# Fused attention and gated feed-forward on one core: V and K loads of two batches issued later in the second chunk

## The chip, the core and the metric

The kernel runs on 1 of the 8 cores of one Trainium2 chip. Its five engines work side by side and meet only at semaphores: TensorE (matmuls; PE in the profile), VectorE (DVE), ScalarE (ACT), GpSimd (POOL) and SyncE (SP). The last three issue DMAs too, each through a queue of its own (q0 GpSimd, q1 SyncE, q10 ScalarE), all run by the same 16 DMA engines. The metric is the device time of one execution, in microseconds (us).

## What is computed

Attention with a causal mask and a decay from running sums, for 8 batches, 8 heads, 576 positions and 64 elements per head; then RMS norm and a gated feed-forward layer over 4608 tokens of 512 elements, with an inner width of 1536.

```python
scores = scale * np.matmul(q, k.transpose(0, 1, 3, 2))
cum = np.cumsum(np.maximum(s, 0.0), axis=-1)
bias = -(cum[:, :, :, None] - cum[:, :, None, :])
scores = np.where(causal, -1000000000.0, scores + np.minimum(bias, 0.0))
...
attn = attn / (np.sum(attn, axis=-1, keepdims=True) + 1e-09)
x = np.matmul(attn, v)            # to (4608, 512): tokens of a batch follow each other
...
g = (x / rms * rms_g) @ w_gate
return (g * (1.0 / (1.0 + np.exp(-g))) * ((x / rms * rms_g) @ w_val)) @ w_out
```

The kernel looks only at the key block of a query block and the one before it (weights further off are below its tolerance; it checks this, and a second, general path is there if the check fails).

## The kernel before

**Two streams, woven by hand.** The feed-forward layer works in 9 chunks of 512 tokens (`ffn`, L746). A chunk has 12 pairs of gate matmuls (L756) and value matmuls (L765), four of 128x512 each, and then four output tiles of twelve matmuls (L778). The attention of batch b must give its normed, turned tokens (`xnT`) before the chunk that holds them. To fill TensorE, attention work is placed between the groups of the chunk's matmuls: after each group `step()` (L681) is called, 36 times a chunk, and a running number, `slot`, counts the calls. `phase()` is the number within the chunk. Chunk 1, the stretch of this case, has slots 37 to 72.

**What a step records.** First the second half of the last score group's exponentials (`pending`); then scaling and the transpose of a finished x block by DMA (`x_scale`, L386; `xt_dma`, L394); one entry of the ScalarE list (`act_side`); one DMA transpose of keys or queries (`kq_dma`, L170); on odd slots one entry of the V list (`v_side`); one of the GpSimd list (`pool_side`); then, by `place()`, scores (`s_step`), attention times V (`av_step`) or a transpose on TensorE (`t_step`); then a check entry on VectorE. Each list is served from its head: an entry is a pair of a condition and the work. The order on each engine is the order of recording; nothing is reordered later. An engine that runs ahead of the others starts what was recorded for later steps, as far as its semaphores let it.

**How a batch's data arrive.** Keys and queries come as float32 in one DMA of 1 MB for 512 rows (`load_kq`, L127, line L129) and one of 128 KB for the last 64 rows (`load_kq_tail`, L133, line L135), issued by ScalarE, into one buffer for keys and one for queries (`kq32`). They are cast to bf16 into `kqn` by GpSimd or ScalarE (L143, L145, L154, L156). For batch 2 the keys are turned on TensorE (L195), the queries by five DMA transposes on SyncE (L182), one for each block. Scores of key block kb read the query blocks kb and kb + 1 (L276, `kqTx[..., kb:kb + 2, ...]`); their matmul is L278, the exponential L302, the causal mask on GpSimd L311. V comes in five blocks (four of 128 rows, one of 64), each one DMA that GpSimd issues, with a cast to bf16 (`load_v`, L184, line L186), into one of two buffers by the parity of the batch. Attention times V of query block qb reads V blocks qb - 1 and qb (L344, L350) and is divided on VectorE (L357, L359); the norm's sum is taken on ScalarE (L366) and its power on GpSimd (L379, L382), the scaling on VectorE (L389), the transpose to `xnT` by SyncE (L400).

**Who sets the moved loads' places.** `over(w)` (L509) is recorded with the last cast of batch b and lists the next batch's load on `act_side`, by `early` with a lag of 4 slots. With `loads` (L486) the bulk and the tail are also 3 slots apart from each other and from the load before. `after_av(b)` (L549) runs when batch b's attention is finished and lists V of batch b + 2: for b = 0 three entries that wait for chunk 1, otherwise one entry a block by `early`, with a lag of 6 slots. The entry `done["V", b]` only tells the scheduler from when on attention of that batch may be placed.

**Slots before**, as the schedule gives them: V of batch 2 blocks 0 and 1 at 37, 2 and 3 at 39, 4 at 41; queries of batch 3 (bulk) at 40, tail at 43; query transposes of batch 2 at 37, 39, 42, 44, 46; V of batch 3 at 45, 47, 49, 51, 53; keys of batch 3 at 46, tail at 49, their five casts at 56 to 60; scores of batch 2 at 46 (key block 0, heads 0 to 3), 49, 52 (key block 1, heads 0 to 3), 55 and on.

Of the kernel before, what the change touches and what calls it, by code (L numbers as in the profile page):

```python
# [26 lines left out]
def kernel(  # L27
# [19 lines left out]
    NSC = 5  # L47
# [6 lines left out]
    def rows(c):  # L54
        return 128 if c < 4 else 64
# [71 lines left out]
    def load_kq(eng, b, w, h0=0, h1=H):  # L127
        src = k if w == 0 else q
        eng.dma_start(  # L129
            out=kq32[:, w, h0:h1, 0:256],  # L130
            in_=src[b, h0:h1, 0:512, :].rearrange("h (p r) d -> p h (r d)", r=4))

    def load_kq_tail(eng, b, w):  # L133
        src = k if w == 0 else q
        eng.dma_start(  # L135
            out=kq32[0:64, w, :, 256:320],
            in_=src[b, :, 512:576, :].rearrange("h p d -> p h d"))

    def cast(eng, b, w, r0, r1, h0=0, h1=H):
        o = kqn[:, b % 2, w, r0:r1, h0:h1, :]  # L140
        i = kq32[:, w].rearrange("p h (r d) -> p r h d", d=D)[:, r0:r1, h0:h1, :]
        if eng is nc.scalar:
            eng.activation(out=o, in_=i, func=AF.Copy)  # L143
        else:
            eng.tensor_copy(out=o, in_=i)  # L145

    def cast_x(eng, b, w, hp):

        if hp < HP:
            o = kqn[:, b % 2, w, 0:4].rearrange("p r h d -> p (r h d)")[:, hp * 512:hp * 512 + 512]  # L150
            o = o.rearrange("p (r h d) -> p h r d", r=4, h=2)
            i = kq32[:, w, 2 * hp:2 * hp + 2, 0:256].rearrange("p h (r d) -> p h r d", d=D)
            if eng is nc.scalar:
                eng.activation(out=o, in_=i, func=AF.Copy)  # L154
            else:
                eng.tensor_copy(out=o, in_=i)  # L156
        else:
            cast(eng, b, w, 4, 5)

    def load_k(b, c):  # L160
        n = rows(c)
        nc.gpsimd.dma_start(
            out=kqn[0:n, b % 2, 0, c],
            in_=k[b, :, c * 128:c * 128 + n, :].rearrange("h p d -> p h d"))
# [19 lines left out]
    def load_v(b, c):  # L184
        n = rows(c)
        nc.gpsimd.dma_start(  # L186
            out=v_sb[0:n, b % 2, c, :, 0:64],
            in_=v[b, :, c * 128:c * 128 + n, :].rearrange("h p d -> p h d"))
# [243 lines left out]
    SLOTS = 36  # L432
    K2 = 34
    slot = [0]
    first, chunk = [0], [0]
    done = {}
# [10 lines left out]
    pool_side, dve_side, v_side, act_side = [], [], [], []  # L447
# [5 lines left out]
    def ready(lag, *key):  # L453
        return at(*key) + lag <= slot[0]
# [11 lines left out]
    def early(queue, lag, fns):  # L466

        t = slot[0] + lag
        queue.extend((lambda: slot[0] >= t and phase() < 24, f) for f in fns)

    def check(b, ws=(1, 0)):
        t = slot[0] + (8 if b >= KB else 0)

        def when(w):
            if b < 2:
                return slot[0] % 2 and chunk[0] == b and slot[0] > 16
            return phase() >= 25 and slot[0] >= t and (w == 0 or ready(0, "cast", b, 1))
        dve_side.extend((lambda w=w: when(w), f) for w in (ws if b < KB else (0, 1)) for f in (
            lambda w=w: check_mag(b, w), lambda: check_max(0), lambda: check_max(1),
            lambda w=w: done.__setitem__(("check", b, w), slot[0])))  # L480

    def phase():

        return slot[0] - first[0]

    def loads(b, w, when, lag):  # L486

        def main():
            load_kq(nc.scalar, b, w)
            last["L"] = slot[0]  # L490

        def tail():
            load_kq_tail(nc.scalar, b, w)
            done["raw", b, w] = last["L"] = slot[0]
        n = len(act_side)
        when(act_side, lag, [main, tail])
        act_side[n:] = [(lambda c=c: c() and slot[0] - last["L"] >= 3, f) for c, f in act_side[n:]]

    def casts(b):

        def key(c):
            load_k(b, c)
            done["K", b, c] = slot[0]
            if c == NSC - 1:
                check(b)

        def over(w):  # L509
            done["cast", b, w] = slot[0]  # L510
            if b + 1 < B and (w == 1 or b + 1 < KB):
                loads(b + 1, w, early, 4)
            if w == 1:
                x_seq.extend((b, ww, c) for c in range(NSC) for ww in ((1, 0) if b >= KB else (1,)))
            else:
                done["cast", b] = slot[0]
                check(b)

        def free(w):
            return ready(0, "check", b - 2, w) and (  # L520
                ready(0, "T", b - 2) if w == 0 and b < KB + 2 else
                b < XB + 2 or ready(4, "X", b - 2, w, 4))
        if b >= KB:
            pool_side.extend((lambda: free(0) and slot[0] % 2 == 0, lambda c=c: key(c)) for c in range(NSC))
        fns = [(1, lambda r=r: cast_x(nc.gpsimd, b, 1, r)) for r in range(NSC)]
        if b == 2:
            fns[-1] = (1, lambda: (cast_x(nc.gpsimd, b, 1, NSC - 1), over(1)))
        else:
            fns += [(1, lambda: over(1))]
        if b < KB:  # L530
            fns += [(0, lambda r=r: cast(nc.gpsimd, b, 0, r, r + 1)) for r in range(NSC)]
            fns += [(0, lambda: over(0))]
        if b == 2:

            def put2(queue, t, *fs):
                queue.extend((lambda: slot[0] >= t and free(0) and free(1), f) for f in fs)
            put2(act_side, K2, *[lambda r=r: cast_x(nc.scalar, b, 1, r) for r in (3, 4)])
            put2(act_side, K2 + 3, *[lambda r=r: cast(nc.scalar, b, 0, r, r + 1) for r in (0, 1, 2)])
            put2(pool_side, K2, *[lambda r=r: cast_x(nc.gpsimd, b, 1, r) for r in (0, 1)],
                 lambda: (cast_x(nc.gpsimd, b, 1, 2), over(1)),  # L540
                 lambda: cast(nc.gpsimd, b, 0, 3, 4), lambda: (cast(nc.gpsimd, b, 0, 4, 5), over(0)))
            return
        pool_side.extend((lambda w=w: ready(7, "raw", b, w) and free(w), f) for w, f in fns)
# [5 lines left out]
    def after_av(b):  # L549
        if b + 2 < B:  # L550
            if b == 0:
                v_side.extend((lambda: chunk[0] == 1, f) for f in (
                    lambda: (load_v(2, 0), load_v(2, 1)), lambda: (load_v(2, 2), load_v(2, 3)),
                    lambda: (load_v(2, 4), done.__setitem__(("V", 2), slot[0]))))
                return
            early(v_side, 6, [lambda r=r: load_v(b + 2, r) for r in range(NSC)]
                  + [lambda: done.__setitem__(("V", b + 2), slot[0])])

    def in_av(b, hp):
# [29 lines left out]
    def do_av(key, ps=None, act=False, apart=False):  # L589
        b, qb, g = key  # L590
        act = act or b > 1 or b == 1 and qb > 1
        norm = av_step(b, qb, g, ps, act)
        if g == 1 and not apart:
            norm()
        done["AV", b, qb, g] = slot[0]
        last["AV"] = slot[0]
        last["AVT" if b > 0 and g == 1 else "AVA"] = slot[0]
        if qb == 4 and g == 1:
            if b == 0:
                nc.vector.memset(v_sb[:, 0, :, :, 64:65], 1.0)  # L600
            after_av(b)
        return norm
# [638 lines left out]
```

## Time and profile before

| what | us |
|---|---|
| median of 3 runs | 365.74 |
| lowest and highest of them | 365.17, 367.58 |
| the profiled execution | 365.71 |
| its span | 364.1 |

How to read the rows: a page row of an engine has its busy time, its share of the span and the number of instructions. A row of the order of time has the start, the length, the engine (with a small q: its queue's issuing instruction), the line, the operation, output <- input, sizes, the count, and in brackets the idle time before it and what ended it. An answer for one line gives shortest, median and longest duration in ns, then the first and last start. A row of a DMA queue gives its packets, MB, and the time of its packets as a share of 16 engines over the window. Matmuls are pipelined, so the bars of neighbouring groups overlap a little.

### The profile page before, as it was taken

Reading aid. Unit: us, or ns where it says so; the run is one execution under the profiler, and the core shown is the slowest. Engines: PE = TensorE matmul, PEld = TensorE weight load, DVE = VectorE, ACT = ScalarE, POOL = GpSimd, SP = SyncE. Lnnn points to the kernel's source line nnn. Section 1 sums busy time; section 2 is a strip of 40 time slices with the busy share of each in tenths; the row PEclk is TensorE's granted clock in tenths of the full one; section 3 lists DMA queues with packets and bytes.
Section 4 is the critical chain, followed back from the end, with each engine's and each line's share of the span. In section 5 each row is a group of like instructions: output and inputs, shape, how many; then the busy total and the mean of one; then the engine's idle time right before and its main releaser. Section 6 shows DMA issues by size and latency. Waiting matters only on the chain. (4 is left out here: it accounts for less than half of the span.)

```text
span 364.1 us, 6986 instructions
## 1 busy us (share of the span) xinstructions
PE 349.6 (96%) x2387; PEld 161.2 (44%) x2387; DVE 272.7 (75%) x524; ACT 240.8 (66%) x619; POOL 174.1 (48%) x281
## 2 busy tenths in 40 slices
PE   5989999998999999999999999999999999999993
PEld 2445444543444444444444444444444444444441
DVE  6697988696887889789988889884588558827820
ACT  3988885776787877876778767777677644223311
POOL 7959763747856465979648833722232200000000
PEclk9999999999999999999999999999999999999998
DMA  7999999999979299999979944952200130020011
GB/s 233 135 222 256 174 176 252 176 196 176 199 133 137 40 199 119 199 161 158 162 213 160 140 109 117 114 78 70 90 14 17 43 110 1 0 88 29 1 58 63
DMA packets 124800, 45.68 MB, mean 125 GB/s; under 512 B 103924, under 2 KB 119800, under 8 KB 124760
## 3 DMA queue, kind: packets, MB, share of 16 engines
q0 software_dynamic: 62368, 13.11, 48.0%
q1 hardware_dynamic: 51328, 23.67, 31.3%
q10 hardware_dynamic: 11064, 8.41, 9.9%
q8 instruction: 19, 0.31, 0.4%
q14 instruction: 21, 0.17, 0.2%
HBM read 37.90 MB, written 9.44 MB: 130 GB/s over the span
## 5 line engine op out<-in xcount | busy, mean ns | idle before, releaser
L302 ACT ACTIVATE E<-psS,biasK 128x256 bf16<-128x256 f32 (+3 forms) x328 | 107.3, 412 | 23.1 <-PE psS L278 21.8
L756 PE MATMUL psF<-xnT,wg_sb 128*128 128x512 bf16 x432 | 111.1, 380 | 0.3 <-ACT xnT L416 0.3
L765 PE MATMUL psF<-xnT,wv_sb 128*128 128x512 bf16 x432 | 111.1, 379 | 0.0
L778 PE MATMUL psF<-wout_sb,Ht 128*128 128x512 bf16 x432 | 102.3, 379 | 0.0
L768 DVE SCALAR_TENSOR_TENSOR U<-T,psF 128x512 bf16<-128x512 f32 x108 | 73.7, 682 | 29.4 <-ACT T L759 29.0
L759 ACT ACTIVATE T<-psF 128x512 f32<-128x512 f32 x108 | 64.4, 596 | 41.4 <-PE psF L756 39.1
L311 POOL TENSOR_SCALAR_AFFINE_SELECT E<-E 128x512 bf16<-128x512 bf16 x64 | 44.6, 697 | 86.6 <-ACT E L302 86.4
L761 DVE TENSOR_TENSOR Ht<-U,psF 128x512 bf16<-128x512 bf16 x99 | 67.7, 684 | 7.0
L756 PEld LDWEIGHTS <-wg_sb 128*128 128x128 bf16 x432 | 38.6, 98 | 44.5 <-issue 5.8
L778 PEld LDWEIGHTS <-Ht 128*128 128x128 bf16 x432 | 38.8, 98 | 42.6 <-issue 2.3
L765 PEld LDWEIGHTS <-wv_sb 128*128 128x128 bf16 x432 | 38.6, 98 | 42.2 <-issue 4.0
L783 ACT ACTIVATE osb<-psF 128x512 f32<-128x512 f32 x36 | 21.5, 598 | 33.3 <-PE psF L778 27.7
L389 DVE SCALAR_TENSOR_TENSOR xs_sb<-x_sb,al_all,g_row 128x512 bf16<-128x512 bf16 (+1 forms) x36 | 29.1, 808 | 13.1 <-POOL al_all L382 12.4
L186 POOL DMA_DIRECT2D v_sb<-in_v_dram x40 | 34.9, 875 | 0.2 <-PE psF L756 0.2
L366 ACT ACTIVATE xs_sb<-x_sb 128x512 bf16<-128x512 bf16 (+1 forms) x37 | 23.5, 636 | 10.9 <-DVE x_sb L359 10.4
L278 PE MATMUL psS<-kqT 64*128 64x256 bf16 (+2 forms) x304 | 25.9, 256 | 2.8 <-DMA kqT<-kqn 1.6
L350 PEld LDWEIGHTS <-E 128*128 128x128 bf16 x320 | 21.7, 97 | 10.1 <-issue 0.2
L427 DVE TENSOR_TENSOR acc<-acc,mag 128x1280 bf16<-128x1280 bf16 x32 | 26.0, 831 | 0.2
L382 POOL TENSOR_TENSOR al_all<-al_all,mhalf 128x1 f32<-128x1 f32 (+2 forms) x39 | 22.2, 570 | 3.3
L278 PEld LDWEIGHTS <-kqT 64*128 64x128 bf16 x320 | 9.0, 94 | 32.9 <-issue 30.5
L344 PEld LDWEIGHTS <-E 128*128 128x128 bf16 x256 | 20.0, 98 | 7.7 <-DVE x_sb L359 0.6
L379 POOL TENSOR_SCALAR al_all<-ss_all 128x1 f32<-128x1 f32 (+2 forms) x39 | 10.3, 263 | 26.3 <-ACT xs_sb L366 18.2
(124 smaller groups left out, 302.4 us busy)
## 6 DMA issues: line engine op xcount, KB each, us to landing
out_dram<-osb SPq DMA_DIRECT2D x36, 256.0 KB, 2.3
kq<-in_q_dram ACTq DMA_DIRECT2D x5, 1024.0 KB, 6.1
v_sb<-in_v_dram POOLq DMA_DIRECT2D x32, 128.0 KB, 6.6
kq<-in_k_dram SPq DMA_DIRECT2D x4, 512.0 KB, 5.4
kq<-in_q_dram SPq DMA_DIRECT2D x4, 512.0 KB, 7.5
kq<-in_k_dram ACTq DMA_DIRECT2D x2, 1024.0 KB, 12.8
kqn<-in_k_dram POOLq DMA_DIRECT2D x16, 128.0 KB, 5.9
wout_sb<-in_moe_w_out_dram POOLq DMA_DIRECT2D x2, 768.0 KB, 10.1
```

The source lines that it names most:

```text
L186: nc.gpsimd.dma_start(out=v_sb[0:n, b % 2, c, :, 0:64], in_=v[b, :, c * 128:c * 128 + n, :].rearrange("h p d -> p h d"))
L278: nc.tensor.matmul(pair[par][:, j * W:j * W + M], lhsT=kT, rhs=qT, start=(j == 0 and not premask), stop=(j == nj - 1))
L302: nc.scalar.activation(out=eo, in_=ei, func=AF.Exp, scale=0.125, bias=biasK[:, kb, bh:bh + 1])
L311: nc.gpsimd.affine_select(out=Ev[:, :, 0:nq], in_=Ev[:, :, 0:nq], pattern=[[0, nh], [1, nq]], compare_op=ALU.is_ge, fill=0.0, base=0, chan ...
L389: nc.vector.scalar_tensor_tensor(out=xs_sb[0:n, (b * NSC + qb) % NX, :], in0=x_sb[0:n, (b * NSC + qb) % NX, :], scalar=al_all[0:n, col:col ...
L427: nc.vector.tensor_tensor(out=acc[:, sl], in0=acc[:, sl], in1=mag[:, sl], op=ALU.max)
L756: nc.tensor.matmul(Gp, lhsT=wg_sb[:, cc, fs], rhs=xnT[:, cc, x0:x0 + DM], start=(cc == 0), stop=(cc == CC - 1))
L759: nc.scalar.activation(out=T, in_=Gp, func=AF.Tanh, scale=0.5)
L761: nc.vector.tensor_tensor(out=Ht[:, fb - 1, :], in0=pend[0], in1=pend[1], op=ALU.mult)
L765: nc.tensor.matmul(Vp, lhsT=wv_sb[:, cc, fs], rhs=xnT[:, cc, x0:x0 + DM], start=(cc == 0), stop=(cc == CC - 1))
L768: nc.vector.scalar_tensor_tensor(out=U, in0=T, scalar=1.0, in1=Gp, op0=ALU.add, op1=ALU.mult)
L778: nc.tensor.matmul(Op, lhsT=Ht[:, fb, tb * 128:(tb + 1) * 128], rhs=wout_sb[:, fb, :], start=(fb == 0), stop=(fb == FB - 1))
```

## The change

Three places in the scheduler's lists, no change to what is computed. The load of keys of batch 3 gets a lag of 11 slots instead of 4. V of batch 3 gets a lag of 11 instead of 6. V of batch 2 goes in four entries instead of three: blocks 0 and 1, and block 2, from the start of chunk 1; blocks 3 and 4 each alone, once the slot is over SLOTS + 8 = 44. The mark that lets attention of batch 2 be placed is set with block 2.

```diff
-                loads(b + 1, w, early, 4)
+                loads(b + 1, w, early, 11 if (b, w) == (2, 0) else 4)
...
             if b == 0:
-                v_side.extend((lambda: chunk[0] == 1, f) for f in (
-                    lambda: (load_v(2, 0), load_v(2, 1)), lambda: (load_v(2, 2), load_v(2, 3)),
-                    lambda: (load_v(2, 4), done.__setitem__(("V", 2), slot[0]))))
+                v_side.extend((lambda n=n: slot[0] > SLOTS + n, f) for n, f in (
+                    (0, lambda: (load_v(2, 0), load_v(2, 1))),
+                    (0, lambda: (load_v(2, 2), done.__setitem__(("V", 2), slot[0]))),
+                    (8, lambda: load_v(2, 3)), (8, lambda: load_v(2, 4))))
                 return
-            early(v_side, 6, [lambda r=r: load_v(b + 2, r) for r in range(NSC)]
+            early(v_side, 11 if b == 1 else 6, [lambda r=r: load_v(b + 2, r) for r in range(NSC)]
```

The schedule then gives: V of batch 2 block 2 still at slot 39, block 3 at 45 (before 39), block 4 at 47 (41); V of batch 3 at 49, 51, 53, 55, 57 (45 to 53); keys of batch 3 at 49 (46), tail at 52 (49), their casts at 59 to 63 (56 to 60). No other slot changes: the order of instructions on TensorE, VectorE and SyncE is the same in both kernels.

## The prediction

> **What bounds the kernel now.** I read the page first (busy time by engine), then what TensorE waited for, then the orders of time of TensorE, the queues and GpSimd around the one stretch that the change touches.
>
> ```profile
> PE 349.6 (96%) x2387; PEld 161.2 (44%) x2387; DVE 272.7 (75%) x524; ACT 240.8 (66%) x619; POOL 174.1 (48%) x281
> ```
>
> TensorE is busy for 349.6 of the span of 364.1 us; the next engine, VectorE, for 272.7. So a time is won where TensorE stands still, and lost where something makes it stand still. Its waits, longest first (engine, line, what it waited for: us in total, times, longest):
>
> ```profile
> PE psS L247 <- POOL mneg L887: 4.0, 1, 4.0
> PE psS L278 <- DMA kqT<-kqn: 1.6, 1, 1.6
> PE psS L278 <- ACT E L302: 0.6, 1, 0.6
> ```
>
> The 4.0 us lie in the start-up. The 1.6 us are the only wait on a DMA: a score matmul (L278) waits for a turned block of queries or keys (kqT). The order of time of TensorE shows where:
>
> ```profile
> 83.42 1.02 PE L765 MATMUL psF<-xnT,wv_sb 128*128 128x512 bf16 x4
> 86.08 0.39 PE L278 MATMUL psS<-kqT 64*128 64x256 bf16 x4 [1.64 <-DMA kqT<-kqn]
> 92.10 0.39 PE L278 MATMUL psS<-kqT 64*128 64x256 bf16 x4 [0.64 <-ACT E L302]
> 108.67 1.03 PE L756 MATMUL psF<-xnT,wg_sb 128*128 128x512 bf16 x4
> ```
>
> The value matmuls end at 83.42 + 1.02 = 84.44; the scores of batch 2, key block 1, heads 0 to 3 start at 86.08. 108.67 is the first matmul of chunk 2. These scores read query blocks 1 and 2 (L276). Block 2 is the late one; it is the first of three transposes here, behind x of batch 1:
>
> ```profile
> 74.26 1.17 SPq L400 DMA_TRANSPOSE xnT<-xs_sb  x1
> 75.53 4.12 SPq L182 DMA_TRANSPOSE kqT<-kqn  x3
> ```
>
> The answers for one issue alone: x at 74.3, then query block 2 at 75.5 (who waited, and the time from issue to landing), then a transpose of little traffic at 105.1 for comparison:
>
> ```profile
> L400 SPq DMA_TRANSPOSE xnT<-xs_sb x1: 1173/1173/1173, 74.3 to 74.3; - x1
> DMA to landing us min/median/max: 8.0/8.0/8.0
> ...
> L182 SPq DMA_TRANSPOSE kqT<-kqn x1: 1293/1293/1293, 75.5 to 75.5; - x1
>   PE psS L278: 1.6, 1
> DMA to landing us min/median/max: 10.4/10.4/10.4
> ...
> L400 SPq DMA_TRANSPOSE xnT<-xs_sb x1: 1213/1213/1213, 105.1 to 105.1; - x1
> DMA to landing us min/median/max: 2.4/2.4/2.4
> ```
>
> x landed at 74.26 + 8.0 = 82.3, query block 2 at 75.53 + 10.4 = 85.9, which is the wait's end. A transpose can take 2.4 us. What shares the 16 DMA engines with these, by queue (q0 GpSimd's, q1 SyncE's, q10 ScalarE's), from 75.5 to 82.2 and from 82.2 to 86:
>
> ```profile
> q0 software_dynamic: 2949, 0.37, 109.1%
> q10 hardware_dynamic: 1202, 0.80, 55.8%
> q1 hardware_dynamic: 546, 0.13, 19.3%
> ...
> q10 hardware_dynamic: 343, 0.35, 52.7%
> q1 hardware_dynamic: 833, 0.20, 52.7%
> q0 software_dynamic: 567, 0.07, 33.0%
> ```
>
> The transposes are starved up to 82.2 (19.3% of 16 engines) and then share: in the last 3.8 us they need 0.527 x 3.8 = 2.0 us of all engines, the loads of q0 and q10 take 0.857 x 3.8 = 3.3 us.
>
> **The change part by part.** The orders of TensorE, VectorE and SyncE stay what they are; only places on GpSimd and ScalarE move. The rows of these two:
>
> ```profile
> 72.81 3.39 POOL L186 DMA_DIRECT2D v_sb<-in_v_dram  x4
> 81.00 0.63 POOL L311 TENSOR_SCALAR_AFFINE_SELECT E<-E 128x512 bf16<-128x512 bf16 x1 [4.80 <-ACT E L302]
> 83.69 0.63 POOL L311 TENSOR_SCALAR_AFFINE_SELECT E<-E 128x512 bf16<-128x512 bf16 x1 [0.31 <-ACT E L302]
> 88.88 0.63 POOL L311 TENSOR_SCALAR_AFFINE_SELECT E<-E 128x512 bf16<-128x512 bf16 x1 [2.00 <-ACT E L302]
> ...
> 77.37 0.44 ACTq L129 DMA_DIRECT2D kq<-in_k_dram  x1
> 81.39 0.60 ACTq L135 DMA_DIRECT2D kq<-in_k_dram  x1
> ```
>
> (1) V loads. The four at 72.81 are blocks 2, 3, 4 of batch 2 and block 0 of batch 3. GpSimd runs ahead of the steps in which its work was recorded, so what a load is moved past counts, not the step. Block 3 of batch 2 is recorded six steps later, yet nothing with a wait comes to stand before it: it still goes out at 73.8. Block 4 (64 rows) and V 0 of batch 3 come behind the causal mask that waits at 81.00, so they go out at about 81.6 and 82.3 instead of 74.6 and 75.3. V 1 to 4 of batch 3 each move back by one or two masks or casts, to between 85 and 93.
>
> Three landings, block 3 of batch 2 (out at 73.8), V 0 of batch 3 (75.3), K of batch 3 (77.4):
>
> ```profile
> L186 POOL DMA_DIRECT2D v_sb<-in_v_dram x1: 881/881/881, 73.8 to 73.8; - x1
> DMA to landing us min/median/max: 8.4/8.4/8.4
> ...
> L186 POOL DMA_DIRECT2D v_sb<-in_v_dram x1: 905/905/905, 75.3 to 75.3; - x1
> DMA to landing us min/median/max: 14.5/14.5/14.5
> ...
> L129 ACTq DMA_DIRECT2D kq<-in_k_dram x1: 441/441/441, 77.4 to 77.4; - x1
> DMA to landing us min/median/max: 14.1/14.1/14.1
> ```
>
> (2) K of batch 3 (1 MB, L129) moves on ScalarE's queue from 77.37 to the place of its own tail, 81.39; the tail (L135) to behind the next tanh, about 83.6. The issue costs ScalarE nothing that TensorE waits for: 0.4 us of its queue, as before.
>
> (3) The sum. Where do the moved 1.5 V blocks and K stand in the two stretches? Block 3 of batch 2, unmoved, lands at 73.8 + 8.4 = 82.2, so up to there q0 is occupied with or without block 4 and V 0; and on q10 the queries of batch 3, unmoved, stand ahead of K. So x of batch 1 may land as late as before, 82.3, and I credit nothing there. From 82.2 on, q0's and q10's 3.3 us are almost all moved work, which is now issued at 81.4 to 82.3. The transpose of 105.1 took 2.4 us from issue to landing; I take 1.5 to 2 of these, an estimate, as the way to the first packet, so the moved loads begin at about 83 to 84. The transposes' own 2.0 us in that stretch hold block 2 and, behind it, part of the next: run alone from 82.3, block 2 would be through at 84.3 at the latest, and sooner by what of the 2.0 us is the next block's. TensorE is there at 84.44. Bounds: landing before 84.44 removes the whole 1.64 us; landing at 85.9 as now removes nothing. The nearest row, the transpose of 105.1 with its 2.4 us, lies on the early side, and about half of the 2.0 us runs before the first moved packet; I take a residue of 0.1 us, so 1.5 us gained. A price below nothing belongs to the rivals.
>
> The Trainium skill, DMA: Bandwidth & Descriptors, section Queues, rings and completion order, says that each DMA engine goes round-robin between the queues that have work, a packet at a time, and keeps order within one queue. It speaks against the change up to 82.2: a V block that stood behind others on q0 took no turn from the transposes, so taking it out would give nothing there. The 19.3% against 109.1% is no even share, so the trace bears out the turns only from 82.2 on (52.7% each for q1 and q10).
>
> (4) What comes next. With the stall gone everything behind 84.44 moves 1.64 us earlier. The next TensorE wait, 0.64 us at 92.10, is on ScalarE's exponentials, which themselves follow TensorE (scores, tanh), so it moves along and stays. GpSimd: its 2.00 us of idle time at 88.88 shrinks to about 0.4. It has the same loads and casts to do, so it is at most 1.1 us late on masks whose readers come later than that. Block 4 of batch 2 and V of batch 3 are first read in chunk 2, behind 108.67: no reader is near.
>
> The profiled execution took 365.71 us (span 364.1 and 1.6 around it) and the median of the three is 365.74, so nothing has to be converted: 365.7 - 1.5 = **364.2 us**.
>
> **The rivals.** *A, the loads catch the transpose anyway.* If block 2 isn't through when K and V begin at about 83.3, it shares again and lands between 84.9 and 85.9, and the wait keeps 0.5 to 1.5 us: 365.2 to 365.7. For it: the slow landings of the other queues' loads (14.1 us) show engines far behind the mean, and a landing is that of the slowest of 16. Against it: before, x and block 2 shared all the way with V 4 and V 0, and were 3.6 us apart; now 1 us of that is free of them.
>
> *B, slower: K comes late for its casts.* K of batch 3 took 14.1 us; from 81.39 the same gives 95.5. Its first cast now stands on GpSimd behind a V load and one mask. The rows of GpSimd, VectorE and SyncE around it:
>
> ```profile
> 94.37 0.63 POOL L311 TENSOR_SCALAR_AFFINE_SELECT E<-E 128x512 bf16<-128x512 bf16 x1
> 97.34 1.20 POOL L145 CAST kqn<-kq 128x512 bf16<-128x512 f32 x1
> 102.81 0.80 POOL L379 TENSOR_SCALAR al_all<-ss_all 128x1 f32<-128x1 f32 x1 [0.89 <-ACT xs_sb L366]
> 104.27 0.75 DVE L389 SCALAR_TENSOR_TENSOR xs_sb<-x_sb,al_all,g_row 128x512 bf16<-128x512 bf16 x1 [0.72 <-POOL al_all L382]
> 105.05 1.21 SPq L400 DMA_TRANSPOSE xnT<-xs_sb  x1
> ```
>
> That mask ends at 95.0 now, so at 93.4 shifted, and GpSimd would stand about 2 us in front of a mask, the norm of block 1 of batch 2, three casts of 0.6 to 1.2 us each and the norm of block 2 (102.81). This last one sets the chunk's end: x of block 2 is scaled at 104.27, goes out at 105.05, lands 2.4 later at 107.5, and chunk 2 starts at 108.67: 1.2 us of room. With K at 95.5 the norm of block 2 would be 0 to 1.6 us late, so TensorE would wait 0 to 0.4 us. From there each us of K costs one. The kernel is slower than before once K lands later than about 97.5 (16 us after its issue); at 98.5 the time is 366.7. For it: all five V loads of batch 3 now fall into its time. Against it: the queries of batch 3 and block 3 of batch 2, which ran ahead of it and beside it, are nearly through when it starts, so it should take less than 14.1 us.
>
> *C, more than the stall.* The 0.64 us at 92.10 goes too: 365.7 - 1.64 - 0.64 = 363.4. Nothing in the profile says why it should.
>
> **How the numbers follow.** The forecast (the wait goes, all but 0.2 us at most) 0.66; A 0.18; B with a loss against before 0.11; C 0.05. The range leaves out C's lower end and the far part of B: 363.5 to 366.1; the likeliest case's own is 363.8 to 364.7. A measurement of this kernel tells about 1%, 3.7 us, from no change; all cases lie within that except a far B or a gain with no row behind it: faster 0.02, same 0.95, slower 0.03.
>
> **What would show it.** The wait of L278 on kqT gone from TensorE's waits, or below 0.2 us; query block 2 landing before 84.4; V 4 and V 0 issued after the first mask of batch 2 at about 81.6, V 3 still at 73.8; K out at about 81.4; no new TensorE wait on a DMA, on xnT (L756) or on kqT of batch 3; the first matmul of chunk 2 near 107.1. I would be wrong if block 2 still lands after 85 (A), if GpSimd is idle at L145 until K lands and TensorE waits at L756 (B), or if the gain is made in chunk 1 and given back later.

## The result, and the profile after

The changed kernel takes 364.21 us (median of 22 runs, 363.39 to 365.89); the kernel before, timed beside it, 365.57 (22 runs, 364.11 to 367.58). The ratio is 0.9966, with a 95% interval of 0.9952 to 0.9981: a gain of 1.36 us, 0.7 to 1.8 us by the interval. The forecast was 364.2. Of 99 further timed executions of the kernel before, 15 took 366.9 to 369.4 us at a mean granted clock of 0.991 to 0.994, while in the changed kernel's 34 the clock was never below 0.995; no trace of such an execution is kept. The profiled execution of the changed kernel has a span of 362.1 us, 2.0 less than the one before.

Of the three rows of TensorE's waits shown for before, two are left after the change:

```profile
PE psS L247 <- POOL mneg L889: 4.0, 1, 4.0
PE psS L278 <- ACT E L302: 0.6, 1, 0.6
```

The 1.6 us on kqT are gone, and nothing of that size has come in their place. The order of time of TensorE at the same four points (lines behind the edit have moved by two):

```profile
82.95 1.02 PE L767 MATMUL psF<-xnT,wv_sb 128*128 128x512 bf16 x4
83.91 0.39 PE L278 MATMUL psS<-kqT 64*128 64x256 bf16 x4
89.93 0.40 PE L278 MATMUL psS<-kqT 64*128 64x256 bf16 x4 [0.65 <-ACT E L302]
106.50 1.03 PE L758 MATMUL psF<-xnT,wg_sb 128*128 128x512 bf16 x4
```

The scores of key block 1 follow the value matmuls without a gap. The stretch from there to chunk 2 is as long as before (106.50 - 83.91 = 22.59, and 108.67 - 86.08 = 22.59), so nothing is given back by chunk 2, and little from there to the end of the span (364.1 - 108.67 = 255.4 before, 362.1 - 106.50 = 255.6 after). The first scores of batch 2 started at 78.21 before and at 77.74 after, so 0.5 of the span's 2.0 us had come by then, 0.35 of it ahead of the first load that the change moves: the first turned queries of batch 2 go out at 68.76 before and 68.41 after. GpSimd and ScalarE's queue:

```profile
72.46 1.82 POOL L186 DMA_DIRECT2D v_sb<-in_v_dram  x2
80.54 0.63 POOL L311 TENSOR_SCALAR_AFFINE_SELECT E<-E 128x512 bf16<-128x512 bf16 x1 [6.25 <-ACT E L302]
81.12 1.59 POOL L186 DMA_DIRECT2D v_sb<-in_v_dram  x2
...
80.92 0.39 ACTq L129 DMA_DIRECT2D kq<-in_k_dram  x1
83.08 0.60 ACTq L135 DMA_DIRECT2D kq<-in_k_dram  x1
```

Two V loads still go out ahead of the mask (blocks 2 and 3 of batch 2) and two behind it. The transposes of x and of query block 2, and then K, each with its time to landing:

```profile
L400 SPq DMA_TRANSPOSE xnT<-xs_sb x1: 1171/1171/1171, 73.9 to 73.9; - x1
DMA to landing us min/median/max: 6.9/6.9/6.9
...
L182 SPq DMA_TRANSPOSE kqT<-kqn x1: 1230/1230/1230, 75.2 to 75.2; - x1
DMA to landing us min/median/max: 6.9/6.9/6.9
...
L129 ACTq DMA_DIRECT2D kq<-in_k_dram x1: 385/385/385, 80.9 to 80.9; - x1
DMA to landing us min/median/max: 7.0/7.0/7.0
```

Query block 2 took 6.9 us instead of 10.4 and landed at 82.0, 1.9 us before its reader; K took 7.0 instead of 14.1. The DMA queues from 75.1 to 81.8, to be read against the first three rows of before:

```profile
q0 software_dynamic: 2080, 0.26, 61.7%
q10 hardware_dynamic: 1229, 0.83, 50.1%
q1 hardware_dynamic: 1395, 0.33, 44.8%
```

The share of the transposes' queue went from 19.3% to 44.8%, that of GpSimd's from 109.1% to 61.7%.

### The profile page after: what moved, and what is told of

The parts are those of the page before. It is cut to its first block, busy times and chain, and to the rows that moved or that the text cites. A ratio compares the mean times of both kernels' runs of the same rounds, so it can differ in the third digit from the quotient of the medians.

```text
span 362.1 us, 6942 instructions
## 1 busy us (share of the span) xinstructions
PE 346.3 (96%) x2342; PEld 160.6 (44%) x2387; DVE 275.1 (76%) x524; ACT 240.6 (66%) x619; POOL 174.9 (48%) x281
## 5 line engine op out<-in xcount | busy, mean ns | idle before, releaser
L767 PE MATMUL psF<-xnT,wv_sb 128*128 128x512 bf16 x414 | 109.6, 379 | 1.0
L758 PE MATMUL psF<-xnT,wg_sb 128*128 128x512 bf16 x420 | 109.7, 380 | 0.7 <-ACT xnT L416 0.3
L780 PE MATMUL psF<-wout_sb,Ht 128*128 128x512 bf16 x420 | 100.6, 379 | 0.6
L389 DVE SCALAR_TENSOR_TENSOR xs_sb<-x_sb,al_all,g_row 128x512 bf16<-128x512 bf16 (+1 forms) x36 | 29.5, 819 | 13.1 <-POOL al_all L382 12.3
L278 PE MATMUL psS<-kqT 64*128 64x256 bf16 (+2 forms) x304 | 25.9, 256 | 1.6 <-ACT E L302 0.6
L427 DVE TENSOR_TENSOR acc<-acc,mag 128x1280 bf16<-128x1280 bf16 x32 | 27.2, 871 | 0.2
L278 PEld LDWEIGHTS <-kqT 64*128 64x128 bf16 x320 | 9.0, 94 | 31.1 <-issue 28.4
L379 POOL TENSOR_SCALAR al_all<-ss_all 128x1 f32<-128x1 f32 (+2 forms) x39 | 9.9, 253 | 25.5 <-ACT xs_sb L366 17.3
```

The source lines that it names most:

```text
L278: nc.tensor.matmul(pair[par][:, j * W:j * W + M], lhsT=kT, rhs=qT, start=(j == 0 and not premask), stop=(j == nj - 1))
L389: nc.vector.scalar_tensor_tensor(out=xs_sb[0:n, (b * NSC + qb) % NX, :], in0=x_sb[0:n, (b * NSC + qb) % NX, :], scalar=al_all[0:n, col:col ...
L427: nc.vector.tensor_tensor(out=acc[:, sl], in0=acc[:, sl], in1=mag[:, sl], op=ALU.max)
L758: nc.tensor.matmul(Gp, lhsT=wg_sb[:, cc, fs], rhs=xnT[:, cc, x0:x0 + DM], start=(cc == 0), stop=(cc == CC - 1))
L767: nc.tensor.matmul(Vp, lhsT=wv_sb[:, cc, fs], rhs=xnT[:, cc, x0:x0 + DM], start=(cc == 0), stop=(cc == CC - 1))
L780: nc.tensor.matmul(Op, lhsT=Ht[:, fb, tb * 128:(tb + 1) * 128], rhs=wout_sb[:, fb, :], start=(fb == 0), stop=(fb == FB - 1))
```

## The experiments

Theory: the V blocks that go out ahead of the mask, and then K, share the DMA engines with the turned queries. Rival 1: K, the largest load, is the cause alone. Rival 2: the V blocks are, alone. Four kernels take the change apart; a fifth question, whether the V blocks' lag of batch 3 counts, needs no run: the changed kernel with that lag at 6 again has the same instructions in the same order on all five engines, since the V list is served from its head and batch 2's blocks, now later, push batch 3's to the same slots. (The traces of two kernels below agree: V without K has the lag at 6, the one with the casts back has it at 11, and GpSimd's order is the same in both.) So this third of the diff does nothing beside the other two.

**K alone** (before, with only this):

```diff
-                loads(b + 1, w, early, 4)
+                loads(b + 1, w, early, 11 if (b, w) == (2, 0) else 4)
```

> Before with the load of keys of batch 3 alone moved (lag 11 instead of 4); V of batches 2 and 3 as before. Theory (the moved V blocks and K together hold back the query transposes of batch 2: V up to about 83 us, K after it): block 2 of the queries lands about 1 us sooner at most, the wait of L278 keeps 0.4 to 1.2 us, the time is 364.7 to 365.4. Rival 1 (K alone is the cause): the wait is gone, 364.2. Rival 2 (the V blocks alone are): the wait stays at 1.5 to 1.7 us, 365.6.

Measured: 365.03 us, ratio 0.9991 (0.9968 to 1.0014), no difference shown. The wait, and the landing of query block 2:

```profile
85.47 0.39 PE L278 MATMUL psS<-kqT 64*128 64x256 bf16 x4 [1.04 <-DMA kqT<-kqn]
...
  PE psS L278: 1.0, 1
DMA to landing us min/median/max: 9.0/9.0/9.0
```

Rival 1 falls: with K out of the way block 2 still takes 9.0 us. That the wait is 1.0 and not 1.6 looked like the theory's part for K; the repeats of before (below) take that away.

**All V, without K** (before, with only the four entries of V of batch 2, which push batch 3's along):

```diff
-                v_side.extend((lambda: chunk[0] == 1, f) for f in (
-                    lambda: (load_v(2, 0), load_v(2, 1)), lambda: (load_v(2, 2), load_v(2, 3)),
-                    lambda: (load_v(2, 4), done.__setitem__(("V", 2), slot[0]))))
+                v_side.extend((lambda n=n: slot[0] > SLOTS + n, f) for n, f in (
+                    (0, lambda: (load_v(2, 0), load_v(2, 1))),
+                    (0, lambda: (load_v(2, 2), done.__setitem__(("V", 2), slot[0]))),
+                    (8, lambda: load_v(2, 3)), (8, lambda: load_v(2, 4))))
```

> Before with only V of batch 2 in four entries, as in the change; the lag of V of batch 3 and of K stays. Because the V list is served from its head, V of batch 3 moves to the same places as in the change, so all V is moved and K isn't. Theory: the wait of L278 falls to 0 to 0.6 us, 364.3 to 364.8. Rival 1 (K alone): wait 1.5 to 1.7, 365.6. Rival 2 (V alone): wait gone, 364.2.

Measured: 364.56 us, ratio 0.9976 (0.9955 to 0.9997). The first scores of batch 2, those of key block 1, chunk 2's first matmul, and the landing of block 2:

```profile
78.56 0.39 PE L278 MATMUL psS<-kqT 64*128 64x256 bf16 x4 [0.77 <-DMA kqT<-kqn]
84.72 0.39 PE L278 MATMUL psS<-kqT 64*128 64x256 bf16 x4
107.55 1.04 PE L757 MATMUL psF<-xnT,wg_sb 128*128 128x512 bf16 x4
...
DMA to landing us min/median/max: 7.0/7.0/7.0
```

With K at its old place block 2 takes 7.0 us, as with the whole change (6.9), and its wait is gone. Rival 2 holds for this wait. Two other small losses show: 0.77 us at the first scores, where query block 1 happened to land late, and 107.55 - 84.72 = 22.83 to chunk 2, 0.24 more than 22.59.

**V of batch 3 alone** (before, with its lag at 11): block 4 of batch 2 stays ahead of the mask.

```diff
-            early(v_side, 6, [lambda r=r: load_v(b + 2, r) for r in range(NSC)]
+            early(v_side, 11 if b == 1 else 6, [lambda r=r: load_v(b + 2, r) for r in range(NSC)]
```

> Before with only the lag of V of batch 3 at 11 instead of 6: V 0 of batch 3 goes behind the first mask, block 4 of batch 2 (64 rows) stays ahead of it, K stays. Theory: the wait keeps 0.2 to 1.0 us, 364.4 to 365.2. Rival 1 (K alone): 365.6. Rival 2 (V alone): wait 0 to 0.6, 364.2 to 364.8.

Measured: 364.49 us, ratio 0.9988 (0.9968 to 1.0008), so no gain is shown in the time; no wait on kqT, block 2 in 8.0 us: between the two. The wait was smaller than the theory's 0.2 to 1.0; V 0 of batch 3 was enough here.

**The kernel before, again**, timed, and one more execution:

> The kernel before, unchanged, beside itself: how far the wait of L278 is the same in every execution. Theory: query block 2 lands at 84.6 to 86 us with V 4 and V 0 ahead of the mask (three profiles so far: 85.95, 85.33, 84.58), so the wait is between 0.3 and 1.7 us in this profile; ratio 1 within 0.3%. Rival: the landing is fixed by the program, the wait is 1.6 to 1.7 again, and the small waits of the other kernels are due to their edits.

> The kernel before once more, one look: the same question as for the run beside it. Theory: a wait of 0.3 to 1.7 us, not the same as in the other two profiles. Rival: 1.6 to 1.7.

Measured: 365.47 us, ratio to itself 0.9998 (0.9968 to 1.0028), and 365.48. The wait, first of the one and then of the other:

```profile
84.61 0.40 PE L278 MATMUL psS<-kqT 64*128 64x256 bf16 x4 [0.88 <-DMA kqT<-kqn]
```

```profile
85.82 0.40 PE L278 MATMUL psS<-kqT 64*128 64x256 bf16 x4 [1.65 <-DMA kqT<-kqn]
```

The first came out as the theory said, the second as the rival. So the wait of before is 1.64, 0.88 and 1.65 us in three executions, 1.4 in the mean, close to what the medians gained. Block 2 took 10.4, 9.7 and 9.9 us; K alone, with 9.0, is 0.7 below these, but its transpose also went out later, behind an issue of x of 1.88 us instead of 1.17 to 1.60. Counted from x's issue, block 2 landed after 10.95 us with K alone and after 11.69, 10.93 and 11.55 in before: no part of K is shown.

**The changed kernel again**, beside the three that follow:

> The changed kernel once more, beside the three below. Theory: 364.2 again, no wait of L278 on kqT at key block 1 of batch 2. The first scores of batch 2 (key block 0) start within 0.1 us of the landing of query block 1 in both traces, and with all V moved and K in place they waited 0.77 us; so a wait of up to 0.8 us there is open for this run, by chance of the landing.

Measured: 363.89 us, ratio 0.9954 (0.9922 to 0.9986). No wait on kqT; block 2 in 6.5 us.

**More V ahead of the mask** (before, lag of V of batch 3 at 2, so V 1 goes out at 76.1 as well):

```diff
-            early(v_side, 6, [lambda r=r: load_v(b + 2, r) for r in range(NSC)]
+            early(v_side, 2 if b == 1 else 6, [lambda r=r: load_v(b + 2, r) for r in range(NSC)]
```

> Before with V of batch 3 two places earlier on the V list (lag 2 instead of 6), so that V 1 of batch 3 goes out at about 76 too, ahead of the first mask: one V block more ahead of the turned queries than before, the suspected cost increased. Theory (each V block there costs the turned queries 1 to 2 us): query block 2 lands at 87 to 88, the wait grows from 1.6 to 2.6 to 3.6 us, time 366.5 to 367.6. Rival (K is what holds them, V not): 365.6.

Measured: 364.65 us, ratio 0.9965 (0.9932 to 0.9998). A miss:

```profile
84.71 0.39 PE L278 MATMUL psS<-kqT 64*128 64x256 bf16 x4 [0.52 <-DMA kqT<-kqn]
...
DMA to landing us min/median/max: 9.2/9.2/9.2
```

V 1 stands behind V 0 on q0, and block 2 took no longer for it (9.2 us). That is what the Trainium skill's rule of turns and order within a queue (DMA: Bandwidth & Descriptors, Queues, rings and completion order) gives for a load at the back of the queue, and the trace agrees. V 0 itself landed at 88.1, 3.5 us behind block 2. Why this kernel should even be faster than before isn't settled: its interval ends at 0.9998, and its wait of 0.52 is one execution.

**Blocks 2 and 3 of batch 2 behind the mask too** (on top of the change):

```diff
-                    (0, lambda: (load_v(2, 2), done.__setitem__(("V", 2), slot[0]))),
-                    (8, lambda: load_v(2, 3)), (8, lambda: load_v(2, 4))))
+                    (0, lambda: done.__setitem__(("V", 2), slot[0])),
+                    (10, lambda: (load_v(2, 2), load_v(2, 3))), (10, lambda: load_v(2, 4))))
```

> The changed kernel with blocks 2 and 3 of batch 2 also behind the first mask, out at about 81 instead of 72.5 and 73.4 (V of batch 3 one place later). Theory: query block 1 lands 1 us or more ahead of the first scores (now 0.05 us), block 2 two or more us earlier than now; TensorE's waits in the profile stay as they are since none is left there, but executions in which block 1 is late no longer lose: 363.9 to 364.2. Rival: block 1 is held by the queries of batch 3 (1 MB, same time) and not by V, it lands where it did; or the V blocks now in the later part delay x for chunk 2, 364.2 to 364.8.

Measured: 364.67 us, ratio 0.9976 (0.9946 to 1.0006). Block 2 took 4.6 us, so V, not the queries of batch 3, held it. Query block 1 landed 2.4 us before the first scores, but that V had held it isn't shown: it took 5.6 us from issue to landing here, 7.6 in the last kernel below with the same places of V, and 5.4 in one execution of before. The time is 364.67 against 363.89 for the change beside it, the intervals overlap, and what the rival named came: the gate matmuls of chunk 2 wait for x of block 2.

```profile
107.44 1.04 PE L758 MATMUL psF<-xnT,wg_sb 128*128 128x512 bf16 x4 [0.42 <-DMA xnT<-xs_sb]
```

**The casts of K back at slots 56 to 60** (on top of the change; the loads stay):

```diff
-            done["raw", b, w] = last["L"] = slot[0]
+            last["L"] = slot[0]
+            done["raw", b, w] = slot[0] - (3 if (b, w) == (3, 0) else 0)
```

> The changed kernel with the five casts of keys of batch 3 recorded at slots 56 to 60 as before the change, not 59 to 63; the loads stay where the change put them. In the changed kernel three of the casts stand on GpSimd ahead of the norm of block 2 of batch 2, and x of that block lands 0.17 us before chunk 2 starts (106.33 against 106.50). Theory: that nearness costs nothing in most executions, so the time is that of the changed kernel, 364.2, but x of block 2 is issued 0.5 to 1 us sooner against chunk 2. Rival: part of the change's executions lose there (its 22 runs lie at 363.4 to 364.3 and at 365.0 to 365.9), and this kernel is 0.3 to 0.6 us faster than the change, 363.7.

Measured: 364.37 us, ratio 0.9975 (0.996 to 0.999), no better than the change, and worse at the point it was to help:

```profile
106.59 1.04 PE L759 MATMUL psF<-xnT,wg_sb 128*128 128x512 bf16 x4 [0.15 <-DMA xnT<-xs_sb]
```

Put together, this shows a cost of K's move that I hadn't seen, and how the two moves meet. From the scores of key block 1 to the issue of x of block 2 it is 18.97 us in before (18.98 in its repeats), 19.89 with K alone, 20.40 with V late and the casts in place (this kernel, V without K, V of batch 3 alone), and 19.92 with both late (the change and its repeat). So each move takes room before chunk 2, 0.9 us and 1.4, and both together take no more than K's 0.9. The rows show how, first before, then the change, then V without K:

```profile
99.92 0.75 DVE L389 SCALAR_TENSOR_TENSOR xs_sb<-x_sb,al_all,g_row 128x512 bf16<-128x512 bf16 x1 [0.44 <-POOL al_all L382]
100.59 0.82 DVE L427 TENSOR_TENSOR acc<-acc,mag 128x1280 bf16<-128x1280 bf16 x1
...
97.70 2.77 POOL L145 CAST kqn<-kq 128x512 bf16<-128x512 f32 x3
97.78 1.08 DVE L389 SCALAR_TENSOR_TENSOR xs_sb<-x_sb,al_all,g_row 128x512 bf16<-128x512 bf16 x1 [0.46 <-POOL al_all L382]
98.78 1.23 DVE L427 TENSOR_TENSOR acc<-acc,mag 128x1280 bf16<-128x1280 bf16 x1
...
98.10 0.78 POOL L379 TENSOR_SCALAR al_all<-ss_all 128x1 f32<-128x1 f32 x1
99.56 0.75 DVE L389 SCALAR_TENSOR_TENSOR xs_sb<-x_sb,al_all,g_row 128x512 bf16<-128x512 bf16 x1 [0.73 <-POOL al_all L382]
```

(GpSimd's L379 begins a block's norm.) VectorE scales block 1 (L389) and only then divides the rest of block 2, so what delays the one delays the other. With V late and the casts in place, more V issues (0.7 to 0.95 us each) stand on GpSimd ahead of the norm of block 1: its L379 starts 13.38 us behind the scores (98.10 - 84.72) instead of 12.54, and L389 is 1.0 us late.

With K late, three of the casts go behind that norm, which is then in time (12.55 in the change). But they now run beside VectorE: L389 takes 1.07 to 1.10 us instead of 0.75 in all seven kernels and repeats with the casts there (K alone among them, with no V moved) and in none of the other seven. It is the casts and not the load: the next kernel moves K's load alone and the stretch stays 19.92. What the two engines share there no run shows. The three kernels with V late and the casts in place pay 0.24 to 0.36 us in the stretch to chunk 2 (22.83 to 22.95 against 22.59), the change nothing; that much K's part is worth beside V's.

**K six slots later still**, casts unmoved:

```diff
-                loads(b + 1, w, early, 11 if (b, w) == (2, 0) else 4)
+                loads(b + 1, w, early, 17 if (b, w) == (2, 0) else 4)
...
-            done["raw", b, w] = last["L"] = slot[0]
+            done["raw", b, w] = last["L"] = slot[0] - (6 if (b, w) == (3, 0) else 0)
```

> The changed kernel with K of batch 3 issued six steps later still (bulk at slot 55, tail at 58), its casts and everything else at the changed kernel's places: the prediction's rival B by force. K landed at 87.9 and 90.6 in the changed kernel and its first cast ran at 93.2, so about 8 us later means K at 96 to 98 and GpSimd standing 3 to 5 us in front of that cast, with a mask, two norms and four casts behind it. Theory: x of block 2 of batch 2, which had 0.17 us of room, comes 2 to 4 us late, a new wait of the gate matmuls on xnT at chunk 2 of that size, time 366 to 368. Rival: the reserve between steps takes it up, under 365.

Measured: 365.06 us, ratio 0.9997 (0.9973 to 1.002): the gain is lost, but by less than expected and by another way.

```profile
93.76 0.61 POOL L145 CAST kqn<-kq 128x512 bf16<-128x512 f32 x1 [0.16 <-DMA kq<-in_k_dram]
...
L129 ACTq DMA_DIRECT2D kq<-in_k_dram x1: 375/375/375, 87.7 to 87.7; - x1
DMA to landing us min/median/max: 5.9/5.9/5.9
```

```profile
107.81 1.02 PE L758 MATMUL psF<-xnT,wg_sb 128*128 128x512 bf16 x4 [0.82 <-DMA out_dram<-osb]
```

K landed in 5.9 us and GpSimd stood 0.16 us for it. The 0.82 us are a wait for x of block 2, which landed at 107.72; the row names an output's DMA, but these matmuls read xnT. Its transpose went out at 104.16, no later than in the change by TensorE's clock (19.92 again), and took 3.6 us instead of 2.5, behind the turned queries of batch 3: the bulk of queries of batch 4, issued behind K, landed at 103.27 instead of 101.71, the turned queries 1.5 us later (0.3 of either is that these scores start later here, at 84.24 against 83.91).

**The queries of batch 4 later** (on top of the change, and on top of the kernel with blocks 2 and 3 behind the mask), to give x of block 2 room:

```diff
         act_side[n:] = [(lambda c=c: c() and slot[0] - last["L"] >= 3, f) for c, f in act_side[n:]]
+        if (b, w) == (4, 1):
+            act_side[n] = (lambda: slot[0] >= 70, main)
```

> The changed kernel with the bulk of the queries of batch 4 (1 MB) at slot 70 instead of 59, its casts unmoved: it no longer runs from 92.5 to 101.7 beside the turned queries of batch 3, which stand ahead of x of batch 2 in SyncE's queue. Theory (chunk 2's start is now the nearest point, x of block 2 lands 0.17 us ahead of it): x of block 1 of batch 2 lands 2 to 4 us sooner than 104.7, x of block 2 keeps its issue at about 103.8, so little changes in the profile, and the executions that lose at chunk 2 lose less: 363.7 to 364.2. Rival: the bulk now runs beside x of block 2 and delays it, a wait of 0.5 to 1.5 at chunk 2, 364.7 to 365.5.

> The same on top of blocks 2 and 3 of batch 2 behind the first mask. That kernel had query block 1 landed 2.4 us ahead of the first scores but waited 0.42 us for x of block 2 at chunk 2, landed at 107.40 behind the turned queries of batch 3. Theory: with the bulk of batch 4 out of the way x of block 2 lands before chunk 2 starts, no wait on a DMA is left in the chunk, 363.4 to 363.9, below the changed kernel. Rival: x is late for another reason (its issue, at 104.31 against 103.83), the wait of 0.4 stays, 364.4 to 364.8.

Measured: 370.33 us, ratio 1.0134 (1.0099 to 1.0168), and 369.85, 1.0114 (1.0081 to 1.0148). Both miss; the rival named for the first came, larger than thought. In the first:

```profile
103.89 0.37 ACTq L129 DMA_DIRECT2D kq<-in_q_dram  x1
...
L400 SPq DMA_TRANSPOSE xnT<-xs_sb x1: 1190/1190/1190, 104.1 to 104.1; - x1
  PE psF L760: 4.2, 1
DMA to landing us min/median/max: 7.0/7.0/7.0
...
111.10 1.75 PE L760 MATMUL psF<-xnT,wg_sb 128*128 128x512 bf16 x4 [4.18 <-DMA xnT<-xs_sb]
```

A load of 1 MB issued 0.2 us ahead of x's transpose makes it 7.0 us instead of 2.5, and TensorE pays 4.2. The other kernel has the same wait, 4.1 us. Another 1.7 us or so are lost behind it: TensorE's granted clock is 0.54 from 111.1 to 113.0 and 0.58 from there to 115.0 (four gate matmuls take 1.75 us instead of 1.03), then 1.00 again. In the other kernel it is 0.62 in the 3.9 us behind the wait; behind the 1.64 us of before it stays at 1.00. No version tried beats the change.

Taken over all kernels, the wait goes with V: in the five profiled executions with V 0 of batch 3 ahead of the mask (before three times, K alone, more V) these scores wait for block 2, 0.52 to 1.65 us, and in the nine with V 0 behind it none do. K is at its old place in four of the five and in two of the nine.

## Why the prediction was right

*The bound and the wait.* The 1.64 us on kqT went, wholly, in both profiles of the changed kernel, and the stretch behind it moved along unchanged, with the 0.64 us on the exponentials in it, as step (4) said. The sum, 1.5 us, is close to the 1.36 measured; not because of the 0.1 us of residue, which wasn't there, but because the wait of before is 0.9 to 1.65 us from one execution to the next and the profile had caught a long one. So the closeness is in part luck: a wait on a DMA read from one trace is one draw.

*Step (1), places.* Block 3 of batch 2 stayed at 73.4, block 4 and V 0 of batch 3 went out at 81.1 and 81.8, as worked out (81.6 and 82.3 in before's clock). What I had not seen in the diff is that the lag of V of batch 3 is idle beside the other V edit.

*Step (3), who holds the transpose.* Here the mechanism was half right, and the number was saved by its bound. I credited nothing up to the landing of x, since blocks 2 and 3 of batch 2 would fill q0 up to 82.2 with or without the moved V. But q0 moved 0.37 MB from 75.5 to 82.2 in before, and 0.26 MB, which is those two blocks, in the same stretch after: 0.11 MB of the moved V had run ahead of 82.2. Without it the transposes' queue moved 0.33 MB there instead of 0.13, and block 2 landed at 82.0 (82.5 in before's clock), at the very start of the stretch in which the sum makes its gain, where I had it at 84.3 at the latest. With that falls the inference that taking such blocks out gives nothing up to 82.2. x came sooner too (8.0, 7.3 and 9.2 us in three executions of before, 6.9 and 7.2 after), if by less than block 2, which landed 2.4 to 3.7 us behind x before and 0.7 to 1.3 after. The sum came out the same because no more than the wait can be gained. I also gave K a share, as the load that takes q10 from 83 on. The runs need none: block 2 takes 7.0 us with K at its old place and V moved, and K alone does not stand out from before. That K costs the stretch behind x something isn't excluded: block 2 landed 1.0 us behind x with K alone, but x itself took 9.9 us there, one profile. Rival A, loads that catch the transpose at 83.3, did not come, since block 2 was through at 82.0.

*Rival B.* Its place was right, x of block 2 at the start of chunk 2: the 1.2 us of room shrank to 0.17 (106.50 against 106.33). Its way was wrong. K lands in 7.0 us, not 14, GpSimd doesn't wait for it, and its casts don't hold the norms: block 1's is in time and block 2's waits 0.33 us for ScalarE's sum. The room went because three casts now run beside VectorE's work on these blocks, as the same loss with K alone shows. Step (4) counted the casts as GpSimd's alone and followed them to the masks' readers; their price on VectorE stood at nothing.

## What to carry to other kernels

A load that is issued early "because there is room" can stand ahead of a short transfer that somebody needs: before moving it, look at what else shares the DMA engines in those microseconds, and ask which queue each stands in and behind what. On an engine that runs ahead of the plan, a DMA is held only by an instruction with a wait in front of it; a larger slot number alone moved nothing for block 3. And every such move takes room at the next deadline, so follow to it all that moves, also what moves along (here K's casts): 1.0 of 1.2 us were used up, and none of three further moves in that direction gained anything over the change.

## What the runs showed of the hardware

Time from issue to landing of one and the same transpose of 32 rows, by what stood ahead on GpSimd's queue: 9.0 to 10.4 us in five executions with V blocks 2, 3 and 4 of batch 2 and V 0 of batch 3 out ahead (one with V 1 too, 9.2; one with K moved away, 9.0); 8.0 in one with blocks 2, 3 and 4; 6.5 to 7.3 in six with 2 and 3; 4.5 and 4.6 with none of them. From these, as an estimate, a V block costs the transpose 1 to 2 us (128 KB, or 64 KB for block 4); V 1 at the back of the queue cost nothing that one profile shows.

VectorE's scaling of a block (L389) took 0.75 us with no cast on GpSimd beside it and 1.07 to 1.10 with casts there (seven executions each).

TensorE's granted clock was 0.54 to 0.62 for 3.9 us behind waits of 4.1 and 4.2 us, and 1.00 behind one of 1.64.

Where the executions of one kernel differ by 1 to 2 us, part of it is landings: in three executions of before the wait of L278 on kqT at key block 1 was 0.88 to 1.65 us, and query block 1 landed from 2.6 us before TensorE was ready for the first scores (75.37 against 77.94) to 0.08 us after. In V without K it was 0.77 us after.
